# Two more units routed alone, a first fp32 step issued earlier, and one tanh held in place: a gated scan with sixteen experts

## The chip, the cores and the metric

The kernel runs on one core of a Trainium2 chip. The metric is the device time of one execution in microseconds (us), smaller is better; a time is the median of three runs. The engines named below are TensorE (PE, with its weight loads as PEld), VectorE (DVE), ScalarE (ACT), GpSimd (POOL) and the queue engine SyncE (SP). Each engine executes its own instructions strictly in program order; an instruction that waits holds up everything behind it on that engine.

## The reference

A gated linear recurrence runs over 4 sequences of 3648 tokens with 256 channels; its 14592 rows then go through 16 experts in 4 groups, each row through the one expert that two argmax steps choose.

```python
sig = 1.0 / (1.0 + np.exp(-f_logit))
f = lower_bound + (1.0 - lower_bound) * sig
h = f[:, t] * h + (1.0 - f[:, t]) * x[:, t]        # for t in range(3648)
x = h.reshape(14592, 256)
g_idx = argmax(x @ w_group); g_w = softmax(x @ w_group)[g_idx]
e_idx = argmax(x @ w_expert[g_idx]); e_w = softmax(...)[e_idx]
out[row] = g_w * e_w * (np.maximum(x[row] @ w1[g, e], 0.0) @ w2[g, e])   # 256 -> 1024 -> 256
```

## The kernel before

The kernel has two phases that overlap. **Phase 1** goes over the tokens in 29 units of 512, numbered from 0 (the sixth unit is unit 5). For each unit ACT computes the gate (`p1_tanh`, one tanh over 128x1024, and `p1_affine`, two half-size affine passes); DVE multiplies gate and input (`p1_gate`) and scans along the tokens, one scan for each of two channel halves (`p1_tb`); PE transposes the result back to token rows (`p1_back`, eight fp32 transposes), which ACT copies to the tile `rows`; and PE forms the router's logits (`p1_router`, `p1_logits`, the ACT copy `Lg`). Units 0 to 3 and from 8 on have tiles named `zt`, units 4 to 7 tiles named `st`.

Then the unit, or a pair of units together, is **routed** (`route_thunks`): a dozen small DVE operations (`mx`, `ge`, `pw`, `pm`, `oh`, `oh16f`) find the expert of each token, ACT computes `ex`, and the ranks follow on PE: `f4x` adds the running offsets (`runoff`) to PSUM, and `f4` multiplies `oh16f` by a triangular matrix and by ones (L417, L418, L420). From PSUM, DVE takes the positions (`sc`, `posi`) and from `ex` the gate weights (`sm`, `se`, `s1`, `s2`, a reciprocal); POOL scatters the rows to the expert lists in DRAM. The table `GROUPS` says how many units are routed together.

**Phase 2** runs expert jobs. Early jobs take the first rows of each expert while phase 1 is still going on; the first three of them (0 to 2) multiply in fp32 (`raw1`, 16 multiplications of 128x256 by line L1041, and `raw2`, L1076). From job 3 on each fp32 product is made of three 16-bit ones (L1063 to L1065, then L1095); between the two layers ACT writes `hh` and DVE `hl` (L1069), and ACT and DVE split the weights into two 16-bit parts (L949, L951).

What sets the order: phase 1 is a list of small functions (thunks). Its start, up to a mark in the list, is issued under a manual schedule of PE, DVE and ACT; at the mark "first", which stands in the loop over units at `u == BEGIN` (6), the preparation of job 0 follows: `keep_warm`, a row of dummy matmuls, then the transposes of its gathered rows `xr` and their copies to `xh` and `xl`. Behind that the thunks are mixed with job steps by due times, and the tile scheduler may reorder; `tc.keep_in_program_order` exempts single instructions:

```python
def pinned(u, ins):
    if 8 <= u <= FAST + 1:
        tc.keep_in_program_order(ins)
...
    with tc.manual_schedule(engines={PE, DVE, Activation}):
        start_macro(len(PLAN))
        bg_to(marks["first"])
        for t in prep_thunks(macros[len(PLAN)][0]):
            t()
```

Of the kernel before, what the change touches and what calls it, by code (L numbers as in the profile page):

```python
# [24 lines left out]
CAPS = [988, 848, 808, 748, 592, 588, 536, 488, 448, 392, 340, 308, 240, 160, 144, 108]  # L25
EXTRA_AT = []
CHOOSE = [3, 4, 6, 6, 8, 8, 10, 12, 14, 16, 18, 20, 22, 24, 26, 26]
GROUPS = [1] * 8 + [2] * 10 + [1]
LAG = 10
PACE = (0, 1, 3, 4, 6, 7, 9, 10)  # L30
FAST = 9
# [9 lines left out]
AHEAD = 3  # L41
STAGED = range(4, 8)
BEGIN = 6
BEHIND = {2: 7, 3: 7}
MT = -(-max(CAPS) // 128)
QUARTERS = (13, 14, 15)
# [6 lines left out]
def gated_scan_moe(ctx: ExitStack, tc, zx, lower, wroute, wexp, out, S):  # L53
# [151 lines left out]
        units[u] = {"z": zt[:, 0], "x": zt[:, 1]}  # L205

    def pinned(u, ins):
        if 8 <= u <= FAST + 1:
            tc.keep_in_program_order(ins)

    def p1_tanh(u):
# [233 lines left out]
    def p1_thunks(us, groups, parts):  # L445
# [54 lines left out]
        for u in us + [us[-1] + 1]:  # L500
            seq = []
            if u <= FAST:
                put(lambda u=u: [p1_load(v) for v in range(2, 8 if u < 8 else u + AHEAD)])
                put(lambda u=u: [p1_load(v) for v in NEXT_AT.get(u, ())])
                ending = u - 1 in ends
                if not ending:
                    put(lambda u=u: p1_ta(u + 1))
                if u > 0:
                    put(lambda u=u: p1_router(u - 1))
                    put(lambda u=u: logits(u - 1))  # L510
                    if u > 1:
                        put(lambda u=u: p1_gate(u))
                put(lambda u=u: p1_tb(u, 0))
                wave(u, 1)
                if ending:
                    bind, bound, (s1, f4x, s2, f3, f4, s6, f5, s7s) = routing(u - 1)
                    if u - 1 == BEHIND[2]:
                        f4.mark = "ranked"
                    put(bind)
                    if u > BEGIN:  # L520
                        back(u - 1)
                    put(lambda u=u: p1_tanh(u + 1))
                    put(s1)
                    put(f4x)
                    if u > 1 and member[u - 2] == member[u - 1]:
                        back(u - 2)
                    put(s2)
                    put(f3)
                    put(f4)
                    wave(u, 1)  # L530
                    put(lambda u=u: p1_affine(u + 1))
                    back(u - 1)
                    put(bound)
                    put(s6)
                    put(f5)
                    for f in s7s:
                        put(f)
                    wave(u, 1)
                elif u > 7:
                    wave(u, 1)  # L540
                    back(u - 1)
                for m in [m for m, v in ROWS_AT.items() if u == v]:
                    f = lambda m=m: early_rows(m)
                    f.mark = m
                    put(f)
                if u == BEGIN:
                    f = lambda: None
                    f.mark = "first"
                    put(f)
                put(lambda u=u: p1_tb(u, 1))  # L550
                wave(u, 1 if u < FAST else 99)
                if u in cuts and u - 1 in ends:
                    put(lambda u=u: place(u))
                if u - 1 in ends:
                    put(lambda u=u: [p1_load(v) for v in LAST_AT.get(u, ())])
                    put(lambda u=u: choose(u))
                if u == FAST:
                    f = lambda: None
                    f.mark = "begun"
                    put(f)  # L560
                    for v in [v for v in sorted(cuts) if v <= FAST and v not in ROWS_AT]:
                        f = lambda v=v: early_rows(v)
                        f.mark = v
                        put(f)
                continue
            if u in us:
                seq += [lambda u=u: (p1_load(u + AHEAD - 1), u + 1 in us and p1_ta(u + 1))]
            if u - 1 in us:
                seq += [lambda u=u: p1_back(u - 1, 0)]
            if u in us:  # L570
                seq += [lambda u=u: p1_tb(u, 0)]
            if u - 1 in us:
                seq += [lambda u=u: p1_router(u - 1)]
                seq += [lambda u=u: p1_back(u - 1, 1)]
            if u in us:
                seq += [lambda u=u: p1_tb(u, 1)]
            if u - 1 in us:
                seq += [lambda u=u: logits(u - 1)]
            for t in seq:
                put(t)  # L580
                slot += 1
                for _ in range(1):
                    if not hold:
                        break
                    f = hold.popleft()
                    if isinstance(f, tuple) and f[0] == "scat":
                        scatq.extend((slot + n, g) for n, g in zip(PACE, f[1]))
                    elif isinstance(f, tuple):
                        lagq.append((slot + LAG, f[1]))
                    else:  # L590
                        put(f)
                while scatq and scatq[0][0] <= slot:
                    put(scatq.popleft()[1])
                while lagq and lagq[0][0] <= slot:
                    put(lagq.popleft()[1])
            if u - 1 in ends:
                grp = ends[u - 1]
                T = sum(unit_range(v)[1] - unit_range(v)[0] for v in grp) // P
                G = {}

                def bind(G=G, first=grp[0]):
                    G.update(cur.pop("G"))
                    G["rows"] = group_rows.pop(first)
                if u <= 13:
                    s1, f4x, s2, f3, f4, s6, f5, s7s = route_thunks(G, T, True)
                    rs = [s1, s2, f3, f4x, None, f4, s6, f5]
                else:
                    s1, s2, s3, s4, s5, s6, s7s = route_thunks(G, T)
                    rs = [s1, s2, s3, None, None, s4, s5, s6]
                rs.append(("scat", s7s))  # L610
                put(bind)
                rs.append(lambda u=u: choose(u))
                if u in cuts:
                    rs.append(lambda u=u: place(u))
                    f = lambda u=u: early_rows(u)
                    f.mark = u
                    rs.append(("lag", f))
                hold.extend(rs)
# [202 lines left out]
    def make_job(kind, idx):  # L821
        j = Job()
        j.kind, j.idx = kind, idx
        j.len = EARLY[idx][1] * P if kind == "A" else CAPS[idx] if kind == "B" else P
        j.tiles = -(-j.len // P)
        j.chunks, j.pieces, j.cols, j.parts = [], [], [], []
        at = 0
        while at < j.len:
            rest = j.len - at
            w = 2 * P if rest > 3 * P else P if rest > 2 * P else rest  # L830
            n = UNIT // w
            j.cols.append([list(range(c, min(KF, c + n))) for c in range(0, KF, n)])
            j.pieces += [(b, min(2 * P, at + w - b)) for b in range(at, at + w, 2 * P)]
            parts, b = [], at
            while b < at + w:
                m = at + w - b
                g = 1 if m > 96 else 2 if m > 32 else 4
                parts.append((b, min(m, P // g), g))
                b += P // g
            j.chunks.append((at, w))  # L840
            j.parts.append(parts)
            at += w
        j.raw = kind == "A" and idx < RAW
        j.wh, j.wl, j.st = {}, {}, {}
        j.hh, j.hl = {}, {}
        j.xh, j.xl = {}, {}
        return j

    def job_e(j):
# [103 lines left out]
    def job_xt(j, pi):  # L953
# [2 lines left out]
        c0 = b0 - j.chunks[ch][0]  # L956
        if j.raw:
            if j.idx == 0:
                keep_warm(bank("m2"), 12)
            j.xh[ch] = mo.tile([P, 2 * P], F32, name="xh", bufs=X_BUFS)  # L960
            j.xl[ch] = mo.tile([P, 2 * P], F32, name="xl", bufs=X_BUFS)
        elif c0 == 0:
# [170 lines left out]
    def first_parts():  # L1133
# [10 lines left out]
            out += [(u, f) for f in fs]  # L1144
        return out

    thunks, marks = p1_thunks(list(range(NU)), GROUPS, first_parts())
    bgq = deque(thunks)
    done = [0]
# [82 lines left out]
    with tc.manual_schedule(engines={mybir.EngineType.PE, mybir.EngineType.DVE, mybir.EngineType.Activation}):  # L1232
        start_macro(len(PLAN))
        bg_to(marks["first"])
        for t in prep_thunks(macros[len(PLAN)][0]):
            t()
    pending = None
    for mi, mac in enumerate(macros):
        if mi < len(PLAN):
# [7 lines left out]
        for j in mac:  # L1247
            for ch in range(len(j.chunks)):
                for cs in j.cols[ch]:
                    m1_step(j, ch, cs)  # L1250
                    left -= len(cs)
                    bg_step(q, left - 2, len(cs))
                for pj, pc in ([pending] if pending else []) + ([(j, ch)] if j.raw else []):
# [75 lines left out]
```

## Time and profile before

| | us |
|---|---|
| median of 3 runs | 759.53 (757.71, 759.53, 759.68) |
| profiled execution, its own time | 758.06 |
| profiled execution, span on the core | 756.30 |
| PE busy in the span | 713.8 (94%) |
| DVE busy | 528.5 (70%) |
| ACT busy | 448.2 (59%) |
| POOL busy | 293.6 (39%) |

The profiled execution took 1.76 us more than the span of its instructions. A busy share over the whole span is an average over stages with different limits, so the rows further down are read by stretches of the span.

### The profile page before, as it was taken

Reading aid. Unit: us, or ns where it says so; the run is one execution under the profiler, and the core shown is the slowest. Engines: PE = TensorE matmul, PEld = TensorE weight load, DVE = VectorE, ACT = ScalarE, POOL = GpSimd, SP = SyncE. Lnnn points to the kernel's source line nnn. Section 1 sums busy time; section 2 is a strip of 40 time slices with the busy share of each in tenths; the row PEclk is TensorE's granted clock in tenths of the full one; section 3 lists DMA queues with packets and bytes.
Section 4 is the critical chain, followed back from the end, with each engine's and each line's share of the span. In section 5 each row is a group of like instructions: output and inputs, shape, how many; then the busy total and the mean of one; then the engine's idle time right before and its main releaser. Section 6 shows DMA issues by size and latency. Waiting matters only on the chain.

```text
span 756.3 us, 21299 instructions
## 1 busy us (share of the span) xinstructions
PE 713.8 (94%) x8063; PEld 633.4 (84%) x8063; DVE 528.5 (70%) x1155; ACT 448.2 (59%) x820; POOL 293.6 (39%) x273
## 2 busy tenths in 40 slices
PE   3669999899999999999999999999999999999995
PEld 1457888778888889989989898989899999999995
DVE  6998779999999976694665646464456466557651
ACT  5667777977778864544545444444445455556552
POOL 3767355657665744522112112222212223123222
PEclk9759999999999999999999999999999999999999
DMA  8988799989998772768877533444436445566520
GB/s 323 399 289 288 256 406 267 391 292 317 334 296 258 246 232 66 216 147 221 180 180 157 138 80 112 92 128 109 121 113 162 112 144 137 164 174 194 173 78 30
DMA packets 101929, 151.62 MB, mean 200 GB/s; under 512 B 61696, under 2 KB 71713, under 8 KB 99008
## 3 DMA queue, kind: packets, MB, share of 16 engines
q1 hardware_dynamic: 87328, 102.88, 47.6%
q0 software_dynamic: 11376, 30.02, 10.9%
q10 hardware_dynamic: 3120, 17.34, 6.5%
q8 instruction: 64, 1.05, 0.6%
q14 instruction: 41, 0.34, 0.2%
HBM read 112.53 MB, written 38.01 MB: 199 GB/s over the span
## 4 chain that ended last, share of the span: by engine, by line
PE 64%; DVE 15%; DMA 7%; issue 5%; ACT 4%; SPq 2%; POOL 1%; POOLq 0%; ACTq 0%; DVEq 0%
PE ps_m L1095 29%; PE ps_m L1063 6%; PE ps_m L1064 6%; PE ps_m L1065 6%; DVE w L951 3%; PE ps_p L1063 3%; DVE h L255 3%; PE ps_p L1064 3%; PE ps_p L1065 3%; DMA xs<-blank 2%; PE ps_p L283 2%; PE ps_m L1076 2%; PE ps_m L1041 2%; DVE hl L1069 2%; ACT w L949 2%
## 5 line engine op out<-in xcount | busy, mean ns | idle before, releaser
L1095 PE MATMUL ps_m<-w,hh 128*128 128x256 f16 (+4 forms) x2512 | 301.6, 250 | 0.5 <-ACT o L1107 0.4
L1095 PE MATMUL ps_m<-w,hl 128*128 128x256 f16 (+4 forms) x1256 | 248.9, 250 | 0.1
L1095 PEld LDWEIGHTS <-hh 128*128 128x128 f16 (+4 forms) x2512 | 183.1, 99 | 21.3 <-issue 2.9
L1063 PE MATMUL ps_m<-xh,w 128*128 128x256 f16 (+12 forms) x750 | 183.4, 257 | 4.8 <-DVE hl L1069 4.4
L392 POOL DMA_INDIRECT xs<-rows,posi x114 | 142.7, 1252 | 111.1 <-ACT rows L287 18.7
L1064 PE MATMUL ps_m<-xl,w 128*128 128x256 bf16 (+12 forms) x750 | 183.4, 257 | 0.3 <-DVE xl L1017 0.3
L1065 PE MATMUL ps_m<-xh,w 128*128 128x256 f16 (+12 forms) x750 | 183.4, 257 | 0.0
L951 DVE TENSOR_TENSOR w<-st,w 128x1024 bf16<-128x1024 f32 x116 | 140.2, 1218 | 56.2 <-ACT w L949 56.1
L1109 POOL DMA_INDIRECT out_dram<-o,info x73 | 85.4, 1170 | 238.7 <-ACT o L1107 213.1
L1069 DVE SCALAR_TENSOR_TENSOR hl<-ps_m,hh 128x512 bf16<-128x512 f32 (+10 forms) x163 | 108.3, 667 | 59.4 <-ACT hh L1068 59.2
L1068 ACT ACTIVATE hh<-ps_m 128x512 f16<-128x512 f32 (+10 forms) x163 | 95.7, 588 | 59.6 <-PE ps_m L1065 58.6
L949 ACT CAST w<-st 128x1024 f16<-128x1024 f32 x116 | 120.1, 1047 | 14.6 <-PE ps_m L1095 9.1
L1064 PEld LDWEIGHTS <-w 128*128 128x128 f16 x1056 | 103.7, 98 | 11.4 <-issue 4.2
L1063 PEld LDWEIGHTS <-w 128*128 128x128 f16 x1056 | 103.6, 98 | 10.2 <-issue 2.3
L1065 PEld LDWEIGHTS <-w 128*128 128x128 bf16 x1056 | 103.6, 98 | 7.7 <-issue 0.7
L1095 PEld LDWEIGHTS <-hl 128*128 128x128 bf16 (+4 forms) x1256 | 98.1, 99 | 9.5 <-issue 0.2
L1109 POOL DMA_INDIRECT out_dram<-o,meta x49 | 54.2, 1106 | 100.2 <-ACT o L1107 92.3
L1107 ACT ACTIVATE o<-ps_m,info 128x256 f32<-128x256 f32 (+4 forms) x73 | 32.2, 443 | 76.4 <-PE ps_m L1095 69.1
L1063 PE MATMUL ps_p<-xh,w 128*128 128x256 f16 (+16 forms) x306 | 72.5, 251 | 0.2 <-issue 0.2
L1065 PE MATMUL ps_p<-xh,w 128*128 128x256 f16 (+16 forms) x306 | 72.5, 251 | 0.0
L1064 PE MATMUL ps_p<-xl,w 128*128 128x256 bf16 (+16 forms) x306 | 72.5, 251 | 0.0
L1069 DVE SCALAR_TENSOR_TENSOR hl<-ps_p,hh 128x512 bf16<-128x512 f32 (+11 forms) x66 | 42.5, 644 | 40.8 <-ACT hh L1068 40.7
(179 smaller groups left out, 814.3 us busy)
## 6 DMA issues: line engine op xcount, KB each, us to landing
st<-in_wexp_dram SPq DMA_DIRECT2D x116, 512.0 KB
zt<-in_zx_dram ACTq DMA_DIRECT2D x16, 1024.0 KB
xs<-blank SPq DMA_DIRECT2D x26, 258.0 KB
zt<-in_zx_dram SPq DMA_DIRECT2D x6, 1024.0 KB
w<-in_wexp_dram SPq DMA_DIRECT2D x12, 512.0 KB
st<-in_zx_dram SPq DMA_DIRECT2D x8, 512.0 KB
xr<-xs SPq DMA_DIRECT2D x12, 258.0 KB
xr<-xs SPq DMA_DIRECT2D x16, 129.0 KB
```

The source lines that it names most:

```text
L255: sn = nc.vector.tensor_tensor_scan(out=h[:, k, c0 - a:c1 - a], data0=ff[:, k, c0 - a:c1 - a], data1=uu[:, k, c0 - a:c1 - a], initial=init ...
L392: sc = nc.gpsimd.indirect_dma_start(out=xs_v[G["t0"] + t][:, :], out_offset=bass.IndirectOffsetOnAxis(ap=R["posi"][:, t:t + 1], axis=0), i ...
L949: nc.scalar.copy(j.wh[i], j.st[i])
L951: nc.vector.tensor_tensor(out=j.wl[i], in0=j.st[i], in1=j.wh[i], op=ALU.subtract)
L1063: nc.tensor.matmul(po, w1_at(j.wh, k, c), xh[:, k], start=(k == 0), stop=False)
L1064: nc.tensor.matmul(po, w1_at(j.wh, k, c), xl[:, k], start=False, stop=False)
L1065: nc.tensor.matmul(po, w1_at(j.wl, k, c), xh[:, k], start=False, stop=(k == KD - 1))
L1068: eviction[0] = nc.scalar.activation(hi, pv, AF.Relu).ins
L1069: nc.vector.scalar_tensor_tensor(out=j.hl[ch][:, cs[0]:cs[-1] + 1, 0:w], in0=pv, scalar=0.0, in1=hi, op0=ALU.max, op1=ALU.subtract)
L1095: nc.tensor.matmul(pm[i * q:i * q + n, 0:dw], h[ch][:, c, ts], w2_at(w, c)[:, i * dw:(i + 1) * dw], start=(c == 0 and s == 0), stop=(c == ...
L1107: nc.scalar.activation(o[s, 0:dw], pm[s, 0:dw], AF.Copy, scale=lt.bitcast(F32)[s, r, 1:2])
L1109: nc.gpsimd.indirect_dma_start(out=out_v[out_n[0]].rearrange("n (g d) -> (n g) d", g=g), out_offset=bass.IndirectOffsetOnAxis(ap=lt[s, r, ...
```

## The change

Four edits are made together. Line numbers of the changed kernel are one to seven larger than those of before (L302 becomes L303, L1041 becomes L1048).

- `GROUPS` has ten single units ahead of the pairs where it had eight: units 8 and 9 are routed one by one, and the number of pairs falls from ten to nine.
- `BACKS = 5` replaces `BEGIN` in one condition: at `u == 6` the transposes and row copies of unit 5 stand ahead of unit 7's tanh and of the ranks.
- The mark "first" moves from behind unit 5's routing to right behind its ranks and unit 7's affine passes, so that job 0's preparation is issued there; a new function `first_step` issues job 0's first multiplications behind unit 6's second scan, and a second mark, "begin", ends the manual schedule. Job 0's dummy matmuls go from 12 to 20.
- `pinned` also holds unit 11 (its tanh, by `p1_tanh`) in program order.

```diff
-GROUPS = [1] * 8 + [2] * 10 + [1]
+GROUPS = [1] * 10 + [2] * 9 + [1]
+BACKS = 5
     def pinned(u, ins):
-        if 8 <= u <= FAST + 1:
+        if 8 <= u <= FAST + 2:
             tc.keep_in_program_order(ins)
...
-                    if u > BEGIN:
+                    if u > BACKS:
                         back(u - 1)
                     put(lambda u=u: p1_tanh(u + 1))
...
                     put(lambda u=u: p1_affine(u + 1))
+                    if u == BEGIN:
+                        f = lambda: None
+                        f.mark = "first"
+                        put(f)
                     back(u - 1)
...
+                put(lambda u=u: p1_tb(u, 1))
                 if u == BEGIN:
+                    put(first_step)
                     f = lambda: None
-                    f.mark = "first"
+                    f.mark = "begin"
                     put(f)
-                put(lambda u=u: p1_tb(u, 1))
...
             if j.idx == 0:
-                keep_warm(bank("m2"), 12)
+                keep_warm(bank("m2"), 20)
...
+    def first_step():
+        j = macros[0][0]
+        j.begun.append((0, j.cols[0][0]))
+        m1_step(j, *j.begun[-1])
...
             t()
+        bg_to(marks["begin"])
...
-                    m1_step(j, ch, cs)
+                    if (ch, cs) not in j.begun:
+                        m1_step(j, ch, cs)
```

Three places of the order show what this does. The first is ACT around unit 5's routing. In the rows `st` behind `Lg` is unit 7's gate, `zt` is unit 11's, `ex` belongs to unit 5's routing and `rows` to unit 5's transposes. Before:

```order
L316 COPY Lg<-ps_p 128x80
L218 ACTIVATE st<-st 128x1024
L218 ACTIVATE zt<-zt 128x1024
L426 ACTIVATE ex<-ge 128x80
L228 ACTIVATE st<-st,mid,half 128x512 x2
L228 ACTIVATE zt<-zt,mid,half 128x512
L285 COPY rows<-ps_p 128x2x256
L287 COPY rows<-tokno 128x4
L285 COPY rows<-ps_p 128x2x256
L435 COPY runoff<-ps_p 128x16
```

The same place of ACT in the changed kernel:

```order
L317 COPY Lg<-ps_p 128x80
L286 COPY rows<-ps_p 128x2x256
L288 COPY rows<-tokno 128x4
L286 COPY rows<-ps_p 128x2x256
L219 ACTIVATE st<-st 128x1024
L427 ACTIVATE ex<-ge 128x80
L229 ACTIVATE st<-st,mid,half 128x512 x2
L288 COPY rows<-tokno 128x4
L1020 COPY xh<-ps_p 128x256
L1020 COPY xl<-ps_p 128x256
L436 COPY runoff<-ps_p 128x16
```

The two row copies went from behind `ex` to ahead of the tanh, unit 11's tanh and affine passes left this place, and job 0's `xh` and `xl` come right behind unit 7's gate.

The second place is PE where job 0 begins, with `ps_p<-h,wr` the router of unit 6 and L418 (L419) the ranks of unit 6. Before:

```order
L302 MATMUL ps_p<-h,wr 32x128
L1007 MATMUL ps_p<-ident,xr 128x128 x3
L302 MATMUL ps_p<-h,wr 32x128 x7
L1041 MATMUL ps_m_993<-xh,w_493 128x256
L315 MATMUL ps_p<-ident,rs 128x128
L283 MATMUL ps_p<-ident,h 128x128 x8
L417 MATMUL ps_p<-runoff,row_136 128x80
L1041 MATMUL ps_m_993<-xl,w_495 128x256
L1041 MATMUL ps_m_993<-xh,w_493 128x256
L418 LDWEIGHTS upto
```

The same place of PE in the changed kernel:

```order
L303 MATMUL ps_p<-h,wr 32x128 x4
L1048 MATMUL ps_m_861<-xh,w_493 128x256
L1048 MATMUL ps_m_861<-xl,w_495 128x256
L1048 MATMUL ps_m_861<-xh,w_493 128x256
L1048 MATMUL ps_m_861<-xl,w_495 128x256
L303 MATMUL ps_p<-h,wr 32x128 x3
L1048 MATMUL ps_m_1026<-xh,w_493 128x256
L1048 MATMUL ps_m_1026<-xl,w_495 128x256
L316 MATMUL ps_p<-ident,rs 128x128
L284 MATMUL ps_p<-ident,h 128x128 x8
L418 MATMUL ps_p<-runoff,row_136 128x80
L1048 MATMUL ps_m_1026<-xh,w_493 128x256
```

Ahead of unit 6's ranks stood three fp32 multiplications of job 0, and now seven.

The third place is where units 10 and 11 are ranked together, shown on PE and on DVE. On PE before, job 2's last multiplications of layer one stand around the ranks (the `128x144` product is `f4x`):

```order
L1041 MATMUL ps_m_1610<-xh,w_981 128x256
L1041 MATMUL ps_m_1610<-xl,w_983 128x256
L1041 MATMUL ps_m_1610<-xh,w_981 128x256
L417 MATMUL ps_p<-runoff,row_136 128x144
L418 LDWEIGHTS upto
L418 MATMUL ps_p<-oh16f,upto 128x128
```

On PE in the changed kernel:

```order
L1048 MATMUL ps_m_1745<-xh,w_997 128x256
L1048 MATMUL ps_m_1745<-xl,w_999 128x256
L1048 MATMUL ps_m_1745<-xh,w_997 128x256
L1048 MATMUL ps_m_1745<-xl,w_999 128x256
L418 MATMUL ps_p<-runoff,row_136 128x144
L419 LDWEIGHTS upto
L419 MATMUL ps_p<-oh16f,upto 128x128
```

All sixteen multiplications of job 2's first layer now stand ahead of these ranks, where eleven did. On DVE before, the same routing (`zt` is the gate of a later unit, `h` its scans in pieces, since a sequence ends inside this unit):

```order
L406 TENSOR_TENSOR oh16f<-oh 128x128
L951 TENSOR_TENSOR w_1515<-st,w_1515 128x1024
L244 SCALAR_TENSOR_TENSOR zt<-zt 128x1024
L255 SCALAR_TENSOR_TENSOR h<-zt,h 128x128
L951 TENSOR_TENSOR w_1522<-st,w_1522 128x1024
L361 TENSOR_REDUCE sm<-ex 128x40
L255 SCALAR_TENSOR_TENSOR h<-zt 128x384
L363 SCALAR_TENSOR_TENSOR se<-sm,oh 128x32
L431 TENSOR_TENSOR sc<-ps_p,oh16f 128x128
```

On DVE in the changed kernel:

```order
L407 TENSOR_TENSOR oh16f<-oh 128x128
L432 TENSOR_TENSOR sc<-ps_p,oh16f 128x128
L434 TENSOR_REDUCE posi<-sc 128x8
L245 SCALAR_TENSOR_TENSOR zt<-zt 128x1024
L256 SCALAR_TENSOR_TENSOR h<-zt,h 128x128
L256 SCALAR_TENSOR_TENSOR h<-zt 128x384
L958 TENSOR_TENSOR w_1616<-st,w_1616 128x1024
L958 TENSOR_TENSOR w_1623<-st,w_1623 128x1024
L362 TENSOR_REDUCE sm<-ex 128x40
```

`sc`, which reads the ranks from PSUM, stands right behind `oh16f`, ahead of a gate and the scan's first pieces that it followed before.

## Rows read from the trace of the kernel before

**Rows 1.** The page's head.

```profile
span 756.3 us, 21299 instructions
```

**Rows 2.** Busy time by stretch: start:end, length, each engine's busy (count), PEclk, DMA share, GB/s.

```profile
52.00:56.60 4.60, 4.60 (x31) 3.87 (x29) 4.51 (x15) 3.37 (x8) 2.14 (x3) 0.50 0.97 335
56.60:118.35 61.75, 61.62 (x452) 50.83 (x451) 50.07 (x124) 46.03 (x98) 34.06 (x28) 1.00 0.87 312
118.35:262.00 143.65, 136.87 (x1394) 118.26 (x1392) 142.06 (x309) 115.60 (x218) 88.52 (x72) 0.99 0.93 305
262.00:740.00 478.00, 476.97 (x5794) 435.11 (x5793) 288.09 (x570) 247.95 (x426) 134.87 (x119) 1.00 0.54 144
```

**Rows 3.** Waits from 118.35 to 262: waiter, what it waited for, us, times, longest.

```profile
PE ps_m L1063 <- DVE hl L1069: 4.2, 6, 1.1
```

**Rows 4.** PE's timeline: start, duration, operation, [idle before it <- releaser].

```profile
48.48 0.71 PE L417 MATMUL ps_p<-runoff,row 1*128 1x80 f32 x2
51.89 0.21 PE L418 MATMUL ps_p<-oh16f,upto 128*128 128x64 bf16 x1 [2.70 <-DVE oh16f L406]
...
52.09 1.95 PE L283 MATMUL ps_p<-ident,h 128*128 128x128 f32 x8
53.83 1.49 PE L292 MATMUL ps_m<-upto,tri 128*128 128x128 bf16 x12
...
57.35 0.70 PE L1041 MATMUL ps_m<-xh,w 128*128 128x256 f32 x2
...
60.30 0.19 PE L418 MATMUL ps_p<-oh16f,upto 128*128 128x64 bf16 x1
...
67.46 0.19 PE L418 MATMUL ps_p<-oh16f,upto 128*128 128x64 bf16 x1
```

**Rows 5.** ACT's timeline around unit 5's routing.

```profile
48.71 1.06 ACT L218 ACTIVATE st<-st 128x1024 f32<-128x1024 f32 x1
...
50.85 0.27 ACT L426 ACTIVATE ex<-ge 128x80 f32<-128x80 f32 x1
...
54.07 0.59 ACT L285 COPY rows<-ps_p 128x512 f32<-128x512 f32 x1 [0.17 <-PE ps_p L283]
```

**Rows 6.** DVE's timeline at unit 5's and unit 6's routing.

```profile
49.35 1.28 DVE L255 TENSOR_TENSOR_SCAN h<-st,h 128x512 f32<-128x512 f32 x1
...
51.76 0.23 DVE L361 TENSOR_REDUCE sm<-ex 128x20 f32<-128x80 f32 x1
...
59.82 0.22 DVE L406 TENSOR_TENSOR oh16f<-oh 128x64 bf16<-128x64 f32 x1
```

**Rows 7.** Forms of the routing's first DVE operation: count, busy, mean ns, idle before.

```profile
L329 DVE TENSOR_REDUCE mx<-Lg 128x40 f32<-128x160 f32 x10 | 3.1, 306 | 4.6 <-ACT Lg L316 4.6
...
L329 DVE TENSOR_REDUCE mx<-Lg 128x20 f32<-128x80 f32 x8 | 1.7, 217 | 0.4 <-ACT Lg L316 0.4
```

**Rows 8.** PE's timeline at the ranks of units 10 and 11.

```profile
104.95 0.51 PE L417 MATMUL ps_p<-runoff,row 1*128 1x144 f32 x2
...
107.19 0.59 PE L1041 MATMUL ps_m<-xh,w 128*128 128x256 f32 x2
107.62 0.59 PE L1041 MATMUL ps_m<-xl,w 128*128 128x256 f32 x2
```

**Rows 9.** DVE's timeline from there to the next pair's routing.

```profile
102.46 1.23 DVE L244 SCALAR_TENSOR_TENSOR zt<-zt 128x1024 f32<-128x1024 f32 x1 [0.19 <-ACT zt L228]
103.79 0.48 DVE L255 TENSOR_TENSOR_SCAN h<-zt,h 128x128 f32<-128x128 f32 x1
...
105.54 0.95 DVE L255 TENSOR_TENSOR_SCAN h<-zt 128x384 f32<-128x384 f32 x1
...
106.49 0.28 DVE L431 TENSOR_TENSOR sc<-ps_p,oh16f 128x128 f32<-128x128 f32 x1
...
120.10 0.31 DVE L329 TENSOR_REDUCE mx<-Lg 128x40 f32<-128x160 f32 x1
```

**Rows 10.** Busy time between the last two rows of group 9, columns as in group 2.

```profile
106.49:120.10 13.61, 13.61 (x97) 11.69 (x96) 12.60 (x30) 10.89 (x21) 10.66 (x8) 1.00 0.92 333
```

More of the change, by code (lines that the diff above doesn't have):

```diff
@@ L846, in make_job @@
         j.xh, j.xl = {}, {}
+        j.begun = []
         return j
```

## The prediction

> **What bounds the kernel now.** I read first the windows, since the average of the page hides that the limit changes. [rows 2] gives three stretches with different owners. From 262 to 740 PE is busy 476.97 of 478.00 us: the tail is a fixed amount of PE work, and whatever start it gets is passed to the end one for one. From 118.35 to 262 it is DVE that has no time to spare, 142.06 of 143.65 busy, 1.59 idle, while PE idles 143.65 - 136.87 = 6.78; of that 4.2 us are six waits of PE for `hl`, the DVE half of an eviction [rows 3]. From 56.6 to 118.35 PE is full again (61.62 of 61.75), and DVE idles 11.68. So two clocks matter: when PE starts its fp32 jobs (first multiplication 57.35, [rows 4]), and when DVE enters its full stretch, for which I take the first operation of the routing of units 12 and 13, at 120.10 [rows 9]. I call this point P. Behind it both orders are alike from about 130, so a P that is late by d ends the kernel late by d, less what the 1.59 idle us give back.
>
> Then I read the timelines at the three places that the order shows changed.
>
> **The start of the fp32 jobs (a gain of 2.6).** Before, PE issues the offsets of unit 5 (48.48, 0.71) and then waits 2.70 us, to 51.89, for `oh16f`; the transposes come behind it (52.09, 1.95), then twelve dummies (1.49, 0.124 each) [rows 4]. The change puts the transposes into that wait: 48.5 to about 50.4, then the offsets to 50.9. The scan of unit 6 that stood at 49.35 inside the routing (1.28, [rows 6]) goes behind the positions, so `oh16f` is done 1.2 earlier and the ranks end at about 51.3 instead of 52.1. The eight more dummies cost 8 x 0.124 = 1.0 at most; they cost nothing here, because PE waits afterwards for that moved scan anyhow. On ACT the second row copy started 1.98 behind the transposes (54.07 - 52.09, [rows 4, 5]), so now at 48.48 + 1.98 = 50.46 and is done at 51.0; unit 7's tanh starts there instead of at 48.71 and takes 1.06 less a little overlap, `ex` starts at 52.0 instead of 50.85 [rows 5]. DVE's `sm` reads `ex`: it starts at 52.2 instead of 51.76 [rows 6]. Some 1.2 us of small operations and 1.2 of scan follow, to 54.6. The fourth router product of the changed order needs this scan, so job 0's first multiplication starts at about 54.75: 57.35 - 54.75 = 2.6 ahead.
>
> **What becomes of the 2.6 by unit 8's ranks (lost).** The ranks wait on PE's own queue for `oh16f` of their unit, and DVE is not earlier. It lost 0.45 at `sm`, has the scan still to do (1.2), is rid of unit 11's gate (1.23, the price of such a row in [rows 9]), and overlaps some 0.3 less; the logits copy on ACT is later with the scan. I get `oh16f` of unit 6 done at 60.8, against 60.04 (59.82 + 0.22, [rows 6]), and the ranks at 60.85 against 60.30 [rows 4]. PE has between 54.75 and there seven multiplications at 0.43 (the distance of two starts, 107.62 - 107.19, [rows 8]), 3.0, and some 1.7 of transposes, router and offsets: 4.7 of 6.1 us. It waits 1.4, and the lead is four multiplications (1.7) less 0.55, that is 1.2. At unit 7's ranks (67.46, [rows 4]) the same count gives three multiplications less 0.45: 0.85. Then units 8 and 9 have ranks of their own where before there was one later pair; at unit 8's, PE has 6.4 us of work for DVE's 7.5, and the new ranks are 0.5 more of PE's work. The lead is gone: PE about 0.3 late from there. If DVE keeps up in spite of this count, the whole 2.6 stays; these are the two ends of this term, -2.6 and +0.3.
>
> **Two single routings for one pair (+2.0 of DVE work, hidden before 118).** A pair's first operation takes 306 ns, a single's 217 [rows 7]: two singles cost 128 ns more here, and the small operations on 16 to 32 elements cost the same for one unit as for two. Summed over the thirteen operations by their forms, two singles take 5.5 and a pair 3.3: 2.2 us, from 1.5 (if they overlap their neighbours as the rows do) to 2.6 (with the run-off's copies); I take 2.0. It lies in the stretch where DVE idles 11.68 [rows 2] and shows at the end only if it pushes P.
>
> **The ranks of units 10 and 11 (+2.2 on PE, then +4.1 at P).** They stand behind all sixteen multiplications of job 2 instead of eleven: 5 x 0.43 = 2.2 later in PE's queue. Before, the offsets started at 104.95 [rows 8] and `sc` on DVE at 106.49 [rows 9]. Now 104.95 + 0.3 + 2.2 = 107.45 and, with the ranks' 0.95, `sc` at about 108.5. And DVE's order makes this cost more: `sc` stood behind a gate (1.23) and two scan pieces (0.48 and 0.95), and some 0.3 of `sm` and `se`; now it stands ahead of them and they queue behind the waiting `sc`. Before, from `sc` to P were 13.61 us with 12.60 busy, 1.01 idle [rows 9, 10]. Now 12.60 + 2.96 = 15.6, and I leave 0.15 of idle: 15.75. P comes at 108.5 + 15.75 = 124.25, which is 4.1 late. Waiting on this P are the weights that DVE splits and the `hl` that PE needs.
>
> **The sum.** The trace is of an execution of 758.06, its span 756.30 [rows 1] and 1.76 around it; the median is 759.53. I put the sum on the middle of both, 758.8. P 4.1 late, less half of DVE's 1.59 idle (0.75): +3.35, which gives **762.1**. The two ends: everything as before at P but with the lead kept, -2.6; P late and PE's clock down again after its waits, below, +4.1 + 2.3 = +6.4.
>
> **A rule beside the rows.** From 52 to 56.6 PE is busy all the time and yet granted 0.50, the lower level of 1.2 GHz; from 56.6 on it has 1.00 [rows 2]. Before that it had waited 2.70 us [rows 4]. The Trainium skill, page "TensorE: Matmul & The Clock Gate", section "What's actually happening", says that the throttled state is the default and that activity releases it. The trace agrees (0.50 after the wait, 1.00 after 4.6 busy us). By that rule the filled wait would bring the release forward, and the time would come out as in the third case below.
>
> **Rivals.** *No measurable change*: PE's waits for unit 6 to 8's ranks are short, since DVE takes them earlier than I count, and the 2.6 lead holds to units 10 and 11. Then the offsets start at 104.95 - 2.6 + 2.2 = 104.55, `sc` at 105.6, P at 121.35 by the same 15.75, 1.25 late; with 0.75 given back +0.5: 759.3. For it: DVE has 11.68 idle. Against it: the `oh16f` that PE waits for come out of a row of dependent steps through ACT, and the row got longer by the two copies. The limit is P: it decides when P is within 2 us of 120.10. *Faster*: filling the wait raises the clock by 52 instead of 56.6; 4.6 us of PE work at 0.50 are 2.3 at 1.00, which pays for the new offsets and waits up to 75, and the full DVE stretch is not work that is in the way but DVE standing between evictions of a PE that is itself ahead. Then the 2.6 reach the end: 758.8 - 2.6 = 756.2. For it: PE idles only 0.13 from 56.6 to 118.35 [rows 2], so a start that is earlier there is worth all of it; against it: DVE's 1.59 idle in 143.65 leave 1 per cent, and the 2.0 of new work is not taken off. It decides when `sc` of units 10 and 11 comes by 104 or so and PE's 6.78 idle do not grow. *The change does not do what it says*: the scheduler issues job 0's step no earlier, because `xh` comes late from ACT; then the lead is nothing, and P is late as forecast; it ends in the first case.
>
> **How the numbers follow.** This kernel's measurement can tell 0.3%, 2.3 us: faster is below 757.25, slower above 761.81. My forecast (P three to five us late) 0.48, its own range 759.5 to 765.5; a part of 0.06 lies under 761.81. The second case 0.32, 758.0 to 761. The faster one 0.20, 755 to 757.2. So faster 0.20, same 0.06 + 0.32 = 0.38, slower 0.42. The range from 756.0 to 765.5 holds the first two and about half of the third.
>
> **What would show each step.** The first L1048 at about 54.8, and a granted clock of 1.00 from then or not. DVE's `sm` of unit 5 waiting for `ex`. PE waits ahead of L419 of units 6, 7 and 8 of about 1.4, 1 and 1; if they are under 0.5, the lead holds and the second or third case is right. `sc` of units 10 and 11 waiting on DVE for PE, at about 108.5, and P at about 124. PE's idle time between 118 and 262, mostly for `hl`, longer than 6.78 by three or four. I am wrong if P is early, or if P is late and PE's tail from 262 is not: then DVE's full stretch is not what sets the end.

## The result, and the profile after

The changed kernel takes 762.83 us (median of six runs, 762.36 to 764.38), the kernel before 758.90 in six runs: 1.0057 times as long, 95% interval 1.0043 to 1.0071. That is slower by 3.9 us, more than the 2.3 us that can be told from no change. Ratios, here and below, need not be the quotient of the medians beside them (here that is 1.0052), and they leave out runs with a clearly lower granted clock (below, one of 1077.13 and one of 795.38). The profiled execution of the changed kernel took 762.95, its span is 761.2.

The windows of the changed kernel over the same stretches as [rows 2], with the same columns:

```profile
52.00:56.60 4.60, 4.49 (x35) 3.39 (x33) 4.11 (x11) 2.50 (x8) 2.85 (x3) 0.75 0.91 228
56.60:118.35 61.75, 58.35 (x418) 47.17 (x416) 49.25 (x135) 44.84 (x95) 27.53 (x24) 1.00 0.85 296
118.35:262.00 143.65, 136.25 (x1388) 117.77 (x1383) 142.45 (x309) 116.71 (x219) 90.49 (x72) 0.99 0.93 308
262.00:740.00 478.00, 476.02 (x5701) 434.42 (x5693) 288.44 (x571) 245.74 (x424) 133.45 (x119) 1.00 0.54 146
```

The stretch from 118.35 on is as full on DVE as before (142.45 against 142.06), and the tail nearly as full on PE (476.02 against 476.97): most of the loss must have been collected ahead of 118.35. PE, which was busy 61.62 of 61.75 us between 56.6 and 118.35, is now busy 58.35.

PE's timeline of the changed kernel at the places of [rows 4] and [rows 8]:

```profile
48.63 1.92 PE L284 MATMUL ps_p<-ident,h 128*128 128x128 f32 x8
50.48 0.71 PE L418 MATMUL ps_p<-runoff,row 1*128 1x80 f32 x2
51.14 0.21 PE L419 MATMUL ps_p<-oh16f,upto 128*128 128x64 bf16 x1
...
51.34 2.29 PE L293 MATMUL ps_m<-upto,tri 128*128 128x128 bf16 x20
...
54.35 0.63 PE L1014 MATMUL ps_p<-ident,xr 128*128 128x128 f32 x3
...
55.44 0.70 PE L1048 MATMUL ps_m<-xh,w 128*128 128x256 f32 x2
...
61.23 0.19 PE L419 MATMUL ps_p<-oh16f,upto 128*128 128x64 bf16 x1
...
68.58 0.19 PE L419 MATMUL ps_p<-oh16f,upto 128*128 128x64 bf16 x1 [0.87 <-DVE oh16f L407]
...
76.41 0.19 PE L419 MATMUL ps_p<-oh16f,upto 128*128 128x64 bf16 x1 [0.76 <-DVE oh16f L407]
...
79.65 0.59 PE L1048 MATMUL ps_m<-xh,w 128*128 128x256 f32 x2
...
99.97 0.59 PE L1048 MATMUL ps_m<-xh,w 128*128 128x256 f32 x2
...
108.20 0.59 PE L1048 MATMUL ps_m<-xl,w 128*128 128x256 f32 x2
108.73 0.51 PE L418 MATMUL ps_p<-runoff,row 1*128 1x144 f32 x2
...
117.83 0.65 PE L303 MATMUL ps_p<-h,wr 128*32 128x128 f32 x16 [1.64 <-DVE xl L1024]
```

The transposes fill the wait of 2.70 before, and the first multiplication comes at 55.44, 1.9 earlier. Then PE waits 0.87 and 0.76 for `oh16f` of units 7 and 8, and the ranks of units 10 and 11 come at 108.73, 3.8 later, directly behind the last of job 2's sixteen multiplications. Job 2 itself (its first multiplication at 99.97) starts 1.5 later than in the kernel before:

```profile
98.46 0.59 PE L1041 MATMUL ps_m<-xh,w 128*128 128x256 f32 x2
```

So of the 3.8, 1.5 is job 2's later start and 2.2 the five multiplications more (5 x 0.43). At 117.83 PE waits once more, 1.64 for `xl`, which DVE makes behind the late `sc`. The three waits, 0.87, 0.76 and 1.64, are what PE's busy time in that stretch has lost (61.62 - 58.35 = 3.27).

ACT and DVE of the changed kernel around unit 5's routing, the places of [rows 5] and [rows 6]. ACT first:

```profile
51.07 1.06 ACT L219 ACTIVATE st<-st 128x1024 f32<-128x1024 f32 x1
52.03 0.26 ACT L427 ACTIVATE ex<-ge 128x80 f32<-128x80 f32 x1
...
55.01 0.37 ACT L1020 COPY xh<-ps_p 128x256 f32<-128x256 f32 x1 [1.23 <-PE ps_p L1014]
```

Then DVE, there and at the ranks of units 10 and 11 and the routing behind them ([rows 9]):

```profile
52.32 0.23 DVE L362 TENSOR_REDUCE sm<-ex 128x20 f32<-128x80 f32 x1 [1.23 <-ACT ex L427]
...
53.55 1.25 DVE L256 TENSOR_TENSOR_SCAN h<-st,h 128x512 f32<-128x512 f32 x1
...
107.10 0.29 DVE L407 TENSOR_TENSOR oh16f<-oh 128x128 bf16<-128x128 f32 x1
109.71 0.29 DVE L432 TENSOR_TENSOR sc<-ps_p,oh16f 128x128 f32<-128x128 f32 x1 [2.31 <-PE ps_p L421]
...
110.24 1.22 DVE L245 SCALAR_TENSOR_TENSOR zt<-zt 128x1024 f32<-128x1024 f32 x1
...
124.16 0.31 DVE L330 TENSOR_REDUCE mx<-Lg 128x40 f32<-128x160 f32 x1
124.39 1.22 DVE L958 TENSOR_TENSOR w<-st,w 128x1024 bf16<-128x1024 f32 x1
125.52 0.32 DVE L332 TENSOR_TENSOR ge<-Lg,mx 128x160 f32<-128x160 f32 x1
```

`sc` waits 2.31 us for the ranks with a gate (at 110.24) queued behind it. The routing of units 12 and 13 starts at 124.16 instead of 120.10. A weight split now stands between its `mx` and its `ge`, so the second operation, `ge`, is the fairer mark: 125.52 against 120.44 before, 5.1 late.

### The profile page after: what moved, and what is told of

Its sections match the earlier page's. It is cut to its first block, busy times and chain, and to the rows that moved or that the text cites. A ratio compares the mean times of both kernels' runs of the same rounds, so it can differ in the third digit from the quotient of the medians.

```text
span 761.2 us, 21334 instructions
## 1 busy us (share of the span) xinstructions
PE 716.9 (94%) x8074; PEld 635.7 (84%) x8074; DVE 531.2 (70%) x1167; ACT 448.2 (59%) x822; POOL 289.9 (38%) x273
## 4 chain that ended last, share of the span: by engine, by line
PE 56%; DVE 14%; DMA 13%; issue 8%; ACT 3%; SPq 2%; POOL 2%; POOLq 0%; ACTq 0%; DVEq 0%
PE ps_m L1102 27%; PE ps_m L1070 6%; PE ps_m L1072 6%; PE ps_m L1071 6%; DVE h L256 3%; DMA xs<-blank 3%; PE ps_p L1070 3%; PE ps_p L1071 3%; DVE w L958 3%; PE ps_p L1072 3%; DMA xs<-rows,posi 2%; DMA st<-in_wexp_dram 2%; DVE hl L1076 2%; DMA zt<-in_zx_dram 2%; POOL out_dram L1116 2%
## 5 line engine op out<-in xcount | busy, mean ns | idle before, releaser
L393 POOL DMA_INDIRECT xs<-rows,posi x114 | 139.8, 1226 | 121.9 <-issue 27.6
L958 DVE TENSOR_TENSOR w<-st,w 128x1024 bf16<-128x1024 f32 x116 | 140.2, 1218 | 53.6 <-ACT w L956 53.5
L1116 POOL DMA_INDIRECT out_dram<-o,info x73 | 83.5, 1144 | 240.6 <-ACT o L1114 214.5
```

Source lines behind the costliest of these rows:

```text
L393: sc = nc.gpsimd.indirect_dma_start(out=xs_v[G["t0"] + t][:, :], out_offset=bass.IndirectOffsetOnAxis(ap=R["posi"][:, t:t + 1], axis=0), i ...
L958: nc.vector.tensor_tensor(out=j.wl[i], in0=j.st[i], in1=j.wh[i], op=ALU.subtract)
L1116: nc.gpsimd.indirect_dma_start(out=out_v[out_n[0]].rearrange("n (g d) -> (n g) d", g=g), out_offset=bass.IndirectOffsetOnAxis(ap=lt[s, r, ...
```

## The experiments

All runs are timed in five rounds beside the kernel before on the same chip. Four kernels ran on a chip on which the kernel before takes 758.64, close to the result; eight ran on chips on which it takes 783.9 and 783.6. They are told apart below, since the two kinds of chip do not show the same limit.

The theory is that of the prediction: **everything behind P is fixed, and P hangs on when `sc` of units 10 and 11 gets its ranks and on what is queued behind it.** Rival one says that the 2 us of new DVE work of the two single routings set the end, wherever they lie. Rival two says that it is the front edit, with its copies ahead of the tanh.

**The ranks earlier, DVE's order untouched.** In the changed kernel, eight multiplications of job 2 are tied behind the ranks:

```diff
             for k, x in enumerate((j.xh[ch], j.xl[ch])):
-                nc.tensor.matmul(pm[:, n * w:(n + 1) * w], ...)
+                with tc.issue_after(ranked[10]) if j.idx == 2 and c >= 4 else ExitStack():
+                    nc.tensor.matmul(pm[:, n * w:(n + 1) * w], ...)
```

> The changed kernel in full, with one addition: the last eight of job 2's sixteen multiplications are issued behind the ranks of units 10 and 11. DVE's order stays that of the changed kernel, row for row; on PE the ranks stand behind eight multiplications and four of the second layer, four fewer than in the changed kernel (1.7 us of PE work). Theory of the prediction (DVE's full stretch starts when sc gets these ranks): sc at about 108.1 instead of 109.71, everything behind it 1.6 earlier, ratio 1.0036 instead of 1.0057. Rival one (the singles' DVE work) and rival two (the front edit): no change, 1.0057.

Measured: 760.44, ratio 1.0027 (1.0015 to 1.0039), 2.3 us of the 3.9 are gone. PE and DVE of this kernel (PE's offsets first):

```profile
106.37 0.51 PE L418 MATMUL ps_p<-runoff,row 1*128 1x144 f32 x2
```

```profile
107.35 0.29 DVE L432 TENSOR_TENSOR sc<-ps_p,oh16f 128x128 f32<-128x128 f32 x1 [1.26 <-PE ps_p L421]
...
123.16 0.32 DVE L332 TENSOR_TENSOR ge<-Lg,mx 128x160 f32<-128x160 f32 x1
```

The ranks come 2.36 earlier than in the changed kernel, `sc` 2.36, `ge` 2.36 (123.16 against 125.52): what the ranks give, P passes on to the last hundredth. Not all of the 2.36 is the edit's: ahead of it this execution was already 0.63 earlier (job 2's first multiplication at 99.34 against 99.97), and the edit's own part is 1.73, the price of four multiplications (4 x 0.43 = 1.72) and near the 1.6 that was expected. `oh16f`, which the ranks read, came 1.29 earlier as well (105.81 against 107.10). Nothing of the singles or of the front edit was taken out, so both rivals, which allowed no change, fall as the whole cause. What is left, 1.0027, is taken up behind the table.

**The hold on unit 11 alone** (in the kernel before):

```diff
-        if 8 <= u <= FAST + 1:
+        if 8 <= u <= FAST + 2:
```

> The hold on unit 11's tanh alone, a second time, since the first interval was wide (1.0026 to 1.0083). Theory of the prediction: ranks of units 10 and 11 2.2 later, ratio 1.0026 at least. Rival one and rival two: 1.000.

Measured: 759.78, ratio 1.0022 (1.0006 to 1.0039). It ran once before this on another chip:

> The kernel of before with unit 11's tanh held in program order and nothing else changed. The ranks of units 10 and 11 now stand behind all sixteen multiplications of job 2 instead of eleven. Theory of the prediction: ranks 2.2 later, sc at about 108.3 instead of 106.49, the routing of units 12 and 13 about 2 late: 760.9, ratio 1.0026. Rival one and rival two: 758.9, ratio 1.000, since neither the singles nor the front edit is in it.

There it took 787.87, ratio 1.0054 (1.0026 to 1.0083). The 1.0026 that was expected lies in the first interval and at the end of the second. Both lie above 1, although neither the singles nor the front edit is in it. The trace of the chip with 758.64 shows the way: the offsets at 107.95 instead of 104.95, and on DVE

```profile
108.93 0.29 DVE L431 TENSOR_TENSOR sc<-ps_p,oh16f 128x128 f32<-128x128 f32 x1 [1.35 <-PE ps_p L420]
...
122.94 0.32 DVE L331 TENSOR_TENSOR ge<-Lg,mx 128x160 f32<-128x160 f32 x1
```

Part of this is no effect of the hold: this execution is 0.79 later than that of before already at unit 6's first scan (48.81 against 48.02), up to which both kernels have the same order.

**The front edit alone** (the changed kernel with the old `GROUPS` and without the hold):

```diff
-GROUPS = [1] * 10 + [2] * 9 + [1]
+GROUPS = [1] * 8 + [2] * 10 + [1]
-        if 8 <= u <= FAST + 2:
+        if 8 <= u <= FAST + 1:
```

> The kernel of before with the front edit alone (transposes and copies of unit 5 ahead of its ranks, job 0's first step early, twenty dummies), units 8 and 9 as a pair, unit 11's tanh not held. The first fp32 multiplication starts about 1.9 earlier. The ranks of units 10 and 11 stand behind fourteen of sixteen multiplications, three more than before (1.3 us). Theory of the prediction: the lead is used up at the ranks of units 6 and 7 by half, the ranks of units 10 and 11 come 0.5 late, 758.9 to 759.6, ratio 1.000 to 1.001. Rival one: 758.9. Rival two (the front edit costs it all): 762.8, ratio 1.0052.

Measured: 759.75, ratio 1.0018 (1.0008 to 1.0027), a little more than was allowed and far from rival two's 1.0052. The way there was not the expected one:

```profile
57.00 0.70 PE L1048 MATMUL ps_m<-xh,w 128*128 128x256 f32 x2 [0.76 <-ACT xh L1020]
...
108.47 0.51 PE L418 MATMUL ps_p<-runoff,row 1*128 1x144 f32 x2
```

The first multiplication is early by 0.35 (57.00 against 57.35), not by 1.9, and the offsets are late by 3.5 us, not by 0.5: job 2 starts 2.2 later than before (100.68 against 98.46), and three more of its multiplications stand ahead (1.3). `sc` follows at 109.45 after a wait of 1.08. As the start was hardly early in this execution, it cannot show what an early start alone is worth at the end.

**The changed kernel without the hold:**

```diff
-        if 8 <= u <= FAST + 2:
+        if 8 <= u <= FAST + 1:
```

> The changed kernel without the hold, a second time, since the first interval (1.0020 to 1.0061) holds both answers. Theory of the prediction: 1.002, since the ranks of units 10 and 11 stand behind eleven multiplications again. Rival one and rival two: 1.0052.

Measured: 762.59, ratio 1.0057 (1.0044 to 1.0070): as slow as the changed kernel, where the theory as I had put it said 1.002. It was tried before that on another chip:

> The changed kernel without the hold on unit 11's tanh (the singles and the front edit stay). The order then has the ranks of units 10 and 11 behind eleven of job 2's sixteen multiplications again, five fewer than in the changed kernel, while sc on DVE still stands right behind oh16f. Theory of the prediction (the late ranks of units 10 and 11 hold up DVE's full stretch): the ranks come 5 x 0.43 = 2.2 earlier, sc starts at about 107.5 instead of 109.71, the routing of units 12 and 13 about 2 earlier than 124.16: 760.7, a ratio of 1.002. Rival one (the extra DVE work of the two singles sets the end, wherever it lies): no change against the changed kernel, 762.8, ratio 1.0052. Rival two (the front edit with its copies ahead of the tanh costs it): also 762.8.

which gave 787.98, ratio 1.0041 (1.0020 to 1.0061). The expectation was wrong and the trace says where. The ranks do stand behind eleven multiplications again, but job 2 starts 2.5 later than in the changed kernel (102.50 against 99.97), mostly because PE waits ahead of it for job 2's rows from DRAM:

```profile
88.93 0.36 PE L1014 MATMUL ps_p<-ident,xr 128*128 128x128 f32 x1 [1.55 <-DMA xr<-xs]
89.73 0.62 PE L1014 MATMUL ps_p<-ident,xr 128*128 128x128 f32 x3 [0.44 <-DMA xr<-xs]
...
108.99 0.51 PE L418 MATMUL ps_p<-runoff,row 1*128 1x144 f32 x2
```

The two waits, 1.99, nearly use up the five multiplications, 5 x 0.43 = 2.15. Why the rows came late is open: they were asked for earlier than in the changed kernel (82.59 against 84.17), whose PE did not wait for them. The offsets come at 108.99 (108.73 in the changed kernel), and DVE:

```profile
109.97 0.29 DVE L432 TENSOR_TENSOR sc<-ps_p,oh16f 128x128 f32<-128x128 f32 x1 [4.38 <-PE ps_p L421]
...
125.92 0.33 DVE L332 TENSOR_TENSOR ge<-Lg,mx 128x160 f32<-128x160 f32 x1
```

`oh16f` started 1.8 us sooner here (105.30), so DVE waits 4.38 instead of 2.31, and ends up at the same place. This speaks for the theory's core (the time of the ranks decides, not how much DVE had done by then) and against my account of which edit makes the ranks late.

**All six profiled executions of this kind of chip side by side** (us; the last column is the span less `ge` of units 12 and 13):

| kernel | job 2 starts | multiplications ahead of the offsets | offsets of 10 and 11 | `sc` | `sc` to `ge` | `ge` | span | behind `ge` |
|---|---|---|---|---|---|---|---|---|
| before | 98.46 | 11 | 104.95 | 106.49 | 13.95 | 120.44 | 756.3 | 635.9 |
| hold alone | 99.30 | 16 | 107.95 | 108.93 | 14.01 | 122.94 | 758.6 | 635.7 |
| front alone | 100.68 | 14 | 108.47 | 109.45 | 14.49 | 123.94 | 759.0 | 635.1 |
| ranks earlier | 99.34 | 8 and 4 of layer two | 106.37 | 107.35 | 15.81 | 123.16 | 757.9 | 634.7 |
| changed | 99.97 | 16 | 108.73 | 109.71 | 15.81 | 125.52 | 761.2 | 635.7 |
| changed, no hold | 102.50 | 11 | 108.99 | 109.97 | 15.95 | 125.92 | 760.9 | 635.0 |

The last column differs by 1.2 us at most, `ge` by 5.5: P decides. (Each row is one execution and goes with its own span, not with the median; those of the hold alone and of the front alone lie 0.6 and 1.1 above theirs.) In every kernel but the first, `sc` follows the offsets by 0.98, since it waits for them. And the column in the middle has two values: about 14 where units 8 and 9 are a pair, 15.8 to 16 where they are single. There `sc` stands right behind `oh16f`, ahead of the gate and the scans that it followed before.

The lateness of `ge` can be counted a second way, by DVE's busy and idle time from unit 6's first scan to `ge`. Before, changed, and ranks earlier (columns as in [rows 2], DVE is the third):

```profile
48.02:120.44 72.42, 69.53 (x507) 57.35 (x511) 60.46 (x151) 54.77 (x115) 41.01 (x34) 0.94 0.87 302
48.32:125.52 77.20, 73.65 (x539) 59.81 (x540) 63.09 (x162) 55.48 (x118) 38.49 (x35) 0.96 0.85 291
47.96:123.16 75.20, 73.34 (x539) 59.82 (x540) 63.12 (x162) 55.12 (x118) 38.99 (x35) 0.96 0.88 299
```

The first two windows hold the same DVE instructions, but that two singles' routings stand in place of one pair's. Of the 5.1 us, 0.3 is the window's later start, 2.6 is that work, and 2.2 is DVE idling more (11.96 before, 14.11 after). With the ranks earlier the idle time is back at 12.08, and the 2.7 of work is what is left. Without the hold the parts are 0.4, 2.7 and 2.3; in the two kernels without the singles there is little or no more work, and as much idling (start, work and idle 0.8, -0.5, 2.2 for the hold alone; 0.8, 0.6, 2.1 for the front alone). So the late ranks are about half of the loss, which a run has shown, and by this count the singles' work is the other half: rival one is wrong as the whole cause and right as a part. The ratios on this chip agree: the front edit alone reads 1.0018, with the singles added (the run without the hold) 1.0057, and the hold on top of both adds nothing, 1.0057. The singles alone were not run on this kind of chip.

**The runs on the other chips.** Two undo or make one part, the units 8 and 9 as a pair in the changed kernel, and the singles alone in the kernel before (each the one line of `GROUPS`):

> The changed kernel with units 8 and 9 routed as a pair again (front edit and hold stay). The ranks of units 10 and 11 stand behind all sixteen multiplications of job 2 and three of its second layer, while on DVE sc stands behind a gate, two weight splits and sm. Theory of the prediction: the ranks stay late, sc at about 108.5, the routing of units 12 and 13 about 2 later than 120.10, 761.0 or a ratio of 1.0027. Rival one (DVE work of the singles): as before, 758.9. Rival two (front edit): 762.8.

Measured: 786.35, ratio 1.0019 (0.9992 to 1.0047): near the theory's 1.0027, under rival two's 1.0052, and not told from rival one's 1.000.

> The kernel of before with units 8 and 9 routed singly and nothing else changed. The ranks of units 10 and 11 stand behind eight of job 2's sixteen multiplications, three fewer than before; sc stands right behind oh16f on DVE. Theory of the prediction: 2 us more of DVE work in a stretch with 11.7 idle, ranks not late: 759 to 760, ratio 1.000 to 1.0015. Rival one (DVE work of the singles sets the end): two thirds or all of the loss, 761.5 to 762.8, ratio 1.0035 or more. Rival two (front edit): 758.9.

> The singles alone, a second time. Ranks of units 10 and 11 behind eight multiplications, sc right behind oh16f. Theory of the prediction: ranks at about 104.2, sc at about 105.5 with a wait below 1, the order behind it 15.8 to the next routing as in the changed kernel: 0.9 late, ratio 1.001. Rival one (DVE work of the singles sets the end): 1.0035 or more. Rival two: 1.000.

Measured: 784.30, ratio 1.0002 (0.9985 to 1.0019), and the second time 784.00, ratio 1.0041 (1.0019 to 1.0063). The first fits the theory and the second rival one; the two intervals meet only at their ends, although the medians lie 0.06% above those of the kernel before both times. So on these chips an interval tells less than it seems to, and what the singles cost alone stays open between nothing and 0.4%.

The next moves `sc` of units 10 and 11 behind unit 14's first scan, in the changed kernel and in that with the singles alone:

```diff
+            scans[u, k] = sn.ins
...
-            V.tensor_tensor(out=sc, in0=pv[:, 0:T], in1=R["oh16"], op=ALU.mult)
+            with tc.issue_after(scans[14, 0]) if G["t0"] == 40 else ExitStack():
+                V.tensor_tensor(out=sc, in0=pv[:, 0:T], in1=R["oh16"], op=ALU.mult)
...
-                    rs = [s1, s2, f3, f4x, None, f4, s6, f5]
+                    rs = [s1, s2, f3, f4x, None, f4, s6] + [None] * (6 if u == 12 else 0) + [f5]
```

> The changed kernel in full, with PE's order up to the ranks of units 10 and 11 untouched (they stay behind all sixteen multiplications), but sc of these units issued on DVE behind unit 14's first scan, so that the gate, the scans, two weight splits and sm fill the wait for the ranks, as they did before the change. Theory of the prediction, now in two halves (late ranks, and DVE's work queued behind the waiting sc): the wait of 2.31 at sc is gone and everything behind it is 2 earlier, ratio 1.0027 to 1.003 instead of 1.0057. If PE's lateness itself sets the end (PE's own work ahead, not DVE), no change: 1.0057. Rival one (DVE work of the singles) and rival two (front edit): 1.0057.

> The singles alone, with sc of units 10 and 11 behind unit 14's first scans as in the run ahead of this. Theory of the prediction: DVE has no wait for ranks there, what is left is the 2 us of more work in a stretch with 11.7 idle: 0.999 to 1.001. Rival one: 1.0035 or more.

Measured: 787.25, ratio 1.0058 (1.0033 to 1.0084), and 786.31, ratio 1.0042 (1.0015 to 1.0068). Both miss the theory's forecast (1.003 at most and 1.001 at most) and fit the rivals'. In both traces the wait at `sc` is gone, and in neither does the time come down. Against the theory this counts less than it seems, because on these chips P is not the only limit. (In the profiled execution of the first, moreover, PE waits 3.26 us for the weights ahead of job 0's first multiplication, far ahead of the edited place.) The windows of 141.5 us from `ge` on, of the changed kernel in the result and of the singles alone on such a chip:

```profile
125.52:267.02 141.50, 133.30 (x1354) 115.35 (x1353) 140.33 (x307) 112.96 (x213) 89.02 (x70) 0.99 0.92 303
```

```profile
125.52:267.02 141.50, 128.87 (x1310) 110.76 (x1310) 134.46 (x295) 109.09 (x205) 80.03 (x66) 1.00 0.90 288
```

DVE, full in the first (140.33), idles 7 us in the second, and PE 12.6. An earlier P could be swallowed there; that it was is not shown. So whether the queue behind `sc` costs its 1.8 us by itself is read from the table and the count behind it, and was not shown by a run of its own.

The last has twelve dummies instead of twenty in the changed kernel:

```diff
-                keep_warm(bank("m2"), 20)
+                keep_warm(bank("m2"), 12)
```

> The changed kernel with twelve dummies instead of twenty. Theory of the prediction: the eight lie ahead of a wait for unit 6's moved scan and for the copies of xh, so the first multiplication starts no earlier: 1.0057, within 0.001. If they lie on the path: about 0.7 to 1.0 us less, 1.0045. If they are what raises the clock, more time than 1.0057.

Measured: 787.85, ratio 1.0067 (1.0035 to 1.0099): no gain is seen; the interval is too wide to tell. Its trace tells more, from the ranks of unit 5 to the first multiplication:

```profile
54.58 0.21 PE L419 MATMUL ps_p<-oh16f,upto 128*128 128x64 bf16 x1
...
56.93 0.91 PE L1014 MATMUL ps_p<-ident,xr 128*128 128x128 f32 x3
...
58.64 0.70 PE L1048 MATMUL ps_m<-xh,w 128*128 128x256 f32 x2
```

That is 4.06 us, against 4.30 with twenty dummies (51.14 to 55.44). The row of twenty takes 2.29, that of twelve 1.44, but the three transposes behind the twelve take 0.91 at a granted clock of 0.50, and those behind the twenty 0.63 at 1.00.

## Why the prediction was right

**The limit.** Right: the time behind P is the same in six kernels to 1.2 us, and the loss of the profiled execution, 761.2 - 756.3 = 4.9, is the lateness of `ge`, 5.1. One sign failed: PE's idle time from 118.35 to 262, which was to grow by three or four, mostly in waits for `hl`, went from 6.78 to 7.40 (the waits for `hl` from 4.2 to 5.6). It grew ahead of that stretch instead, from 0.13 to 3.40 between 56.6 and 118.35.

**The first multiplication, -2.6.** Measured -1.9, 55.44. The step that was off is that PE would have nothing to do but wait for the moved scan. That scan was done at 54.80, but PE was busy with dummies until 53.6 (51.34 + 2.29) and with the `xr` transposes until 55.0 (54.35 + 0.63), and `xh` was copied only then, ACT waiting 1.23 for them. That the eight dummies, which I put at nothing, are the whole 0.7 is not shown: without them the way to the first multiplication was 0.24 shorter (4.06 against 4.30, in the run with twelve). The other steps there hold: `ex` at 52.03 (52.0), `sm` at 52.32 waiting for it (52.2).

**The lead lost by unit 8's ranks.** Right in kind. PE waits 0.87 and 0.76 at units 7 and 8, where I had 1 and 1; at unit 6, where I had 1.4, the trace marks no wait, although its ranks come 0.9 later (61.23 against 60.30). The size was too small: job 1's first multiplication starts at 79.65, against 78.55 before, and job 2's at 99.97 against 98.46, so PE is 1.1 and then 1.5 late, not 0.3.

**The singles' DVE work, +2.0.** From unit 6's first scan (48.02 before, 48.32 after) to `ge` of units 12 and 13, the windows shown with the experiments have DVE busy for 60.46 us before and 63.09 after, 2.6 more. I had the work hidden in the idle time unless it pushed P. It was not hidden: none of the 11.96 was used up, and the 2.6 is in P.

**The ranks, +2.2 on PE and +4.1 at P.** `sc` was to come at 108.5 and came at 109.71, by PE's larger lateness. I counted 15.75 us from `sc` to `mx`; it took 14.45, because the weight split that I had ahead of `mx` went behind it. The two errors cancel, 124.16 against 124.25. By the mark `ge`, which is not touched by that, P is 5.1 late, of which 3.2 is `sc` and 1.9 the queue behind it. The five more multiplications are 2.2 of the ranks' 3.8 in the changed kernel, and job 2's later start is 1.5; taking the five away does not bring the ranks forward when job 2 starts later still (the run without the hold).

**Given back, 0.75.** DVE had none to give: in the 141.5 us behind `ge` it is busy 139.95 before and 140.33 after. Against this, the median of the six runs of before turned out 0.8 above its profiled execution, so that the median moved by 3.9 and not by 4.9. The path (late ranks, a late `sc`, DVE's queue behind it, then a fixed remainder) was forecast and was found; that 762.1 comes within 0.8 of 762.83 is in part luck, since a P that was put 1 us too early and 0.75 that was not given back were partly made up by this difference of executions.

**The faster rival.** Its first half happened: the clock is granted at 0.75 in the mean from 52 to 56.6, where it was 0.50, the lower of its two levels, before; a finer reading puts the rise to 1.00 at 54.35, 2.25 earlier, after PE had been busy without a gap from 48.37:

```profile
53.43:54.35 0.92, 0.92 (x6) 0.31 (x4) 0.92 (x3) 0.35 (x2) 0.00 (x0) 0.50 1.09 276
54.35:56.60 2.25, 2.14 (x17) 1.65 (x17) 2.21 (x4) 0.72 (x3) 1.88 (x2) 1.00 0.79 191
```

This agrees with the Trainium skill, page "TensorE: Matmul & The Clock Gate", section "What's actually happening", that activity releases the throttle. The second half did not happen: DVE was not earlier (`oh16f` of unit 6 at 60.96 against 59.82), PE spent its lead in the waits at units 7 and 8, and `sc` came at 109.71 and not by 104.

## What to carry to other kernels

A lead on one engine is worth nothing until the next place where that engine waits for another; count both engines up to there before a gain is put down. Idle time of an engine is no room for more work as long as it lies in waits that the work does not overlap: here 2.6 us more of DVE work went in beside 12 us of idle time, and the idle time stayed. Where a later stretch is full on one engine, look for the first instruction of that engine which waits ahead of it: when its input comes, and what is queued behind it, sets the end. And moving units into other groups or holding one instruction reorders the scheduler's choices far behind the edit: here an edit to units 8, 9 and 11 acted through where the ranks of units 10 and 11 landed among another job's multiplications.

## What was not expected of the hardware

The same kernel, the one before, takes 758.6 us on one chip and 783.6 and 783.9 on two others, with its runs there spread over 778.7 to 787.6 where they lie within 756.6 to 760.0 on the first. In the eight profiled executions on the slower chips the time behind `ge` is 653 to 660 us instead of 635 to 636, and in the 141.5 us behind `ge`, in which DVE is otherwise busy 140, it is busy 129 to 134. What holds them up the traces do not name, and it stays open.
